# Background transfers kept back around a block exchange, and a high/low split placed later, in a one-core convolution and mixer kernel

## Chip, core and metric

The kernel runs on one core of a Trainium2 chip. The core has five engines with a queue each: TensorE (matmuls), VectorE, ScalarE, GpSimd and SyncE. SyncE only issues DMAs; GpSimd here mostly does so too. An engine takes its instructions in order and waits at the head of its queue. The metric is the device time of one execution, in microseconds (us); lower is better.

## The reference

Input `x` has 8 batches of 4096 tokens with 192 channels. A causal convolution with 7 softmax-normalised taps per head (8 heads of 24 channels) is followed by a token mixer and a channel mixer:

```python
w = softmax(weight)                        # 8 heads x 7 taps
xc = sum_k w[h, k] * x_pad[:, s + k, h, :]   # 6 zero rows ahead of each batch
xt = xc.transpose(0, 2, 1)
h = maximum(xt @ w_tok1, 0) @ w_tok2       # 4096 -> 256 -> 4096 tokens
u = xc + h.transpose(0, 2, 1)
out = u + maximum(u @ w_ch1, 0) @ w_ch2    # 192 -> 1536 -> 192 channels
```

## The kernel before

**Groups and tiles.** The batches form five groups, `[0], [1], [2, 3], [4, 5], [6, 7]`. A group's convolution and first token product ("stage 1", `stage1`) run as background while earlier groups go through the rest. The rest is done in tiles of 512 tokens (four blocks of 128), eight tiles a group. Products are made from high and low parts (a rounded copy and the remainder), so most operands exist as a `hi`/`lo` pair.

**A tile of a group of two batches.** For each of its batches (`i` = 0, 1), `channel1` makes 1536 hidden rows for the 512 tokens: six pairs of PSUM banks, 18 matmuls a pair (L971), each bank turned by ScalarE into a high part (L1010) and by VectorE into a low part (L1011). Then channel2 (`channel2_halves` for batch 0, `channel2` for batch 1) makes four output blocks; VectorE adds them to `u` (L1034/L1036, L1049/L1050), and `store_out` sends the tile (L1057, GpSimd's queue). All of these take PSUM banks from one pool of six, `ps_x`, so a bank that VectorE frees late stops the matmul that needs it next.

**The turn.** Within the second batch of a tile the next tile is prepared. After `channel1`, `mix2` makes the second token product of the next tile; VectorE adds it to `u` (L886) and transposes 32x32 blocks (L887). `blocks_sent` then moves these blocks between partitions with 16 DMAs of 48 KB (L920), eight from SyncE's queue and eight from GpSimd's. `parted` waits for them: ScalarE casts the high part (L933, three instructions), VectorE makes the low part (L935, three), ScalarE copies both to the upper half of `other` (L938, two), and GpSimd's queue copies the lower halves (L940, two DMAs). The first channel1 of the next tile reads the first four results at once; the DMA'd halves are read by the second batch's channel1. Before the change, `parted` stands between the second and the third of channel2's four blocks. There are 24 such turns: the last tile of group 1 and all tiles of groups 2 to 4 but the very last.

**The background.** A planner (`Background`) weaves stage 1 into this program at the time it is written. It keeps two estimated clocks, `pe` and `dve`, in nanoseconds. Each foreground step calls `bg.fg(pe, dve, after)`: it advances `pe`, pops background items in `fill` until the estimated VectorE clock is more than `after` ahead of TensorE's, then charges the step's own VectorE time. An item has a cost, a lag behind the item before it, and a gate that can hold it back. Its place in the program is thus decided by estimates, and the engines keep that order whatever the real times are.

**Stage 1 of a pair of batches.** It goes in four sections of 1024 tokens (`q2` = 0 to 3). Each section's rows are loaded in two halves of the channels (`begin`, `load`: two DMAs of 672 KB on SyncE's queue at L622; for section 0 also a memset by GpSimd behind each load, L624). The taps are VectorE instructions over 24 channels (L634, in twos), with the first tap a scale on ScalarE (L632). `store` sends the result with two DMAs on GpSimd's queue (L658). Mixing splits the result (L706 ScalarE, L710 VectorE) and multiplies it on TensorE into `ps_a` (L726 to L728). A section's first tap has a gate: its rows must be marked as loaded, some microseconds must have gone by on the estimated clock (10,000 ns for section 0, else 6,000 for two batches), and the split of the section two before must have been popped. The first half of the next section is loaded while the second half of this one is convolved, and the second half after that.

```python
def begin(q2, part):
    states[q2]["raw", part] = load(q2, part)
    mark("load", q2, part)

def loaded(q2, part):
    at = done.get(("load", q2, part))
    return None if at is None or pools(q2 % 2) is None else at + (2e3 + 2e3 * nb if q2 else 10e3)
```

Of the kernel before, what the change touches and what calls it, by code (L numbers as in the profile page):

```python
# [15 lines left out]
GROUPS = [[0], [1], [2, 3], [4, 5], [6, 7]]  # L16
# [18 lines left out]
class Background:  # L35
# [6 lines left out]
    def __init__(self):  # L42
        self.streams = []
        self.tiled = False
        self.pe = 0.0
        self.dve = 0.0

    def add(self, items, lead=0.0, group=None):
        total = sum(it.cost for it in items) or 1.0
# [53 lines left out]
        self.pe = max(self.pe, self.dve)  # L103

    def finish(self, group=None):
        mine = [s for s in self.streams if s["group"] == group]
        while any(s["items"] for s in mine):
            for s in mine:
                while self.may(s):
                    self.pop(s)  # L110
        self.streams = [s for s in self.streams if s["items"]]
# [3 lines left out]
def conv_mixer_kernel(ctx: ExitStack, tc: tile.TileContext, x, weight, w_tok1, w_tok2, w_ch1, w_ch2, out):  # L115
    nc = tc.nc
# [17 lines left out]
    RB = 8  # L134
# [7 lines left out]
    def f32(ap):  # L142
# [8 lines left out]
    bg = Background()  # L151
# [10 lines left out]
    xcd = [  # L162
        dram.tile([P, len(g), NJ, D], F32, name=f"xcd{i}") for i, g in enumerate(GROUPS)
    ]
# [434 lines left out]
    def stage1(gi, pools):  # L599
        bs = GROUPS[gi]  # L600
        nb = len(bs)
# [36 lines left out]
        states = [{} for _ in range(NS)]  # L638
        done = {}

        def mark(*key):
            done[key] = max(bg.pe, bg.dve)

        def begin(q2, part):
            states[q2]["raw", part] = load(q2, part)
            mark("load", q2, part)

        def taps(q2, h, k):
            st = states[q2]
            if k == 0 and h == 0:  # L650
                st["xc"] = pools(q2 % 2).tile([P, RB * nb, D], F32, name=f"xc{q2 % 2}")
            for i in range(2):
                conv(st["raw", h // HH], st["xc"], h + i, k)

        def store(q2):
            xc = states[q2]["xc"].rearrange("p (j b) d -> p j b d", b=nb)
            for i in range(nb):
                nc.gpsimd.dma_start(out=xcd[gi][:, i, q2 * RB:(q2 + 1) * RB], in_=xc[:, :, i])  # L658
            mark("conv", q2)

        def t1_load(n):
# [176 lines left out]
    def tokens(u, i):  # L838
        return u[:, :, :, i]

    def rows(v):
        return v.rearrange("p (c d) -> p c d", d=D2)
# [193 lines left out]
                nc.vector.tensor_tensor(out=osb[:, j], in0=v, in1=osb[:, j], op=ALU.add)  # L1036
        bg.tiled = False

    def channel2(i, h, u, osb, js):
        for j in js:  # L1040
            ts = slice(j * P, (j + 1) * P)
            ps = ps_x.tile([P, TT], F32, name="ps_x")
            for n, f in enumerate(order):
                z = n == NF - 1
                nc.tensor.matmul(out=ps[:, :2 * D], lhsT=h["hh", f][:, ts], rhs=w2[:, f, :], start=n == 0, stop=False)  # L1045
                nc.tensor.matmul(out=ps[:, :D], lhsT=h["hl", f][:, ts], rhs=w2[:, f, :D], start=False, stop=z)  # L1046
                if n % 4 == 3:
                    bg.fg(1140, 660 if z else 0, 200)
            nc.vector.tensor_tensor(out=rows(osb[:, j]), in0=rows(ps[:, :D]), in1=tokens(u, i)[:, j], op=ALU.add)  # L1049
            nc.vector.tensor_tensor(out=osb[:, j], in0=ps[:, D:2 * D], in1=osb[:, j], op=ALU.add)  # L1050

# [110 lines left out]
    for gi, bs in enumerate(GROUPS):  # L1162
        nb = len(bs)
        last = gi + 1 == len(GROUPS)
        if gi == 0:
            starts[1] = stage1(1, lambda k: sp0)
            starts[1][0](sp0)
            first_items()
        elif not last:
            if gi + 1 not in starts:  # L1170
                starts[gi + 1] = stage1(gi + 1, lambda k: cps[k])
            starts[gi + 1][0](sp)
        if gi == 0:
            u, abc = first["u"][1], first["abc"]
            loaded = first["next"]
        for q in range(NT):
            nxt = (gi, q + 1) if q + 1 < NT else (gi + 1, 0)
            for i, b in enumerate(bs):
                turn = i == nb - 1 and nxt[0] < len(GROUPS)
                run_ahead(gi)  # L1180
                if turn and nxt[0] != gi:
                    starts[nxt[0]][1]()
                    if gi == 0:
                        stage_ctx.close()
                        t2s_ctx.close()
                        conv_pool(1)
                        sp = ctx.enter_context(tc.tile_pool(name="sp1", bufs=1, reuse_waits="tile"))
                    loaded = load_tile(*nxt, sp)
                half = range(0, TJ // 2), range(TJ // 2, TJ)
                ahead = gi or q  # L1190
                if ahead:
                    h = channel1(abc[i])
                    run_ahead(gi)
                    osb = hp.tile([P, TJ, D], F32, name="osb")
                else:
                    osb = first["osb"]
                    first_channel2(u, osb, half[0])
                pairs = len(GROUPS[min(nxt[0], len(GROUPS) - 1)]) > 1
                if turn and pairs:
                    z = up.tile([P, ND * NQ, P], F32, name="own_hi")  # L1200
                    mix2(*nxt, *loaded, turned=z)
                    other = blocks_sent(z)
                elif turn:
                    if gi == 0 and nxt[0] == 0:
                        bg.require(("t2", nxt[1] // 2, nxt[1] % 2))
                    mix2(*nxt, *loaded)
                    mixed[0] = nxt[1]
                product2 = channel2 if turn or last and q + 1 == NT and i + 1 == nb else channel2_halves
                if ahead:
                    product2(i, h, u, osb, half[0])  # L1210
                if turn:
                    abc = parted(other) if pairs else transposed(loaded[1])
                run_ahead(gi)
                if not ahead:
                    w2_split()
                if last and q + 1 == NT and i + 1 == nb:
                    for j in range(TJ):
                        if j in half[1]:
                            channel2(i, h, u, osb, [j])
                        store_out(gi, b, q, osb, range(j, j + 1), nc.sync)  # L1220
                else:
                    if ahead:
                        product2(i, h, u, osb, half[1])
                    else:
                        first_channel2(u, osb, half[1])
                    store_out(gi, b, q, osb, range(TJ), nc.gpsimd)
                if not ahead:
                    ht_ctx.close()
                    hp = ctx.enter_context(tc.tile_pool(name="hp", bufs=1, reuse_waits="tile"))
                if turn:  # L1230
                    u = loaded[1]
                    if nxt[1] + 1 < NT:
                        loaded = load_tile(nxt[0], nxt[1] + 1, sp)
# [31 lines left out]
```

## Time and profile before

| | |
|---|---|
| runs shown (us) | 2060.33, 2061.2, 4994.83 |
| median | 2061.2 |
| profiled execution, its own time | 2060.38 |
| its span in the profile | 2058.6 |
| DMA moved | 258.39 MB, mean 126 GB/s |
| raw-row loads (L622) | 56, median 7.0 us from issue to landing |
| convolution stores (L658) | 28, median 8.1 us |
| block DMAs (L920) | 384, median 2.2 us on SyncE's queue, 2.0 on GpSimd's |
| lower halves (L940) | 48, median 3.5 and 4.9 us |

The span is the time from the first instruction to the last, and 1.8 us of the execution's own time lie around it. Groups 0 and 1 take about the first 600 us. The tiles of groups 2 to 4 follow; stage 1 of groups 3 and 4 runs beside the first twelve or so of them, to about 1380 us, and the tiles after that have no background at all.

In the rows quoted below, `x` and a number give how many instructions a group holds. A time-order row reads: start and duration in us, engine (SPq is SyncE's queue), line, operation, `out<-in`, shapes, and in brackets how long the engine stood idle before it and what ended that. A row of waits reads: who waited for whom, us in total, times, longest. A row of stretches reads: from and to, length, then for TensorE's matmuls, its weight loads, VectorE, ScalarE and GpSimd the busy time and the number of instructions, then TensorE's granted clock (1.00 is full), the DMA engines' busy share and GB/s.

### The profile page before, as it was taken

The page shows a single profiled execution, that of the slowest core. Times are in us where ns is not written, and L with a number is a line of the kernel's source. Part 1 is how long each engine was busy: PE and PEld are TensorE (multiplying, and loading weights), DVE is VectorE, ACT ScalarE, POOL GpSimd, SP SyncE. Part 2 cuts the span into 40 slices and gives each one's busy share as a digit, 9 for nine tenths or more (in the row PEclk, how much of TensorE's full clock was granted, in tenths as well). Part 3 has the DMA queues.
Part 4 walks back from the last instruction along what each step waited for, and adds up shares of the span by engine and source line. Part 5 has one row for each costly group of instructions (what it writes and reads, how often), then busy time and mean ns, then how long its engine had stood idle before and what let it go on. Part 6 is the DMA issues. An engine that isn't in the chain of part 4 may idle for free.

```text
span 2058.6 us, 41998 instructions
## 1 busy us (share of the span) xinstructions
PE 2030.5 (99%) x17435; PEld 1885.0 (92%) x17435; DVE 1450.9 (70%) x2877; ACT 761.2 (37%) x1305; POOL 218.7 (11%) x383
## 2 busy tenths in 40 slices
PE   9999999999999999999999998999999999999999
PEld 9789999998989888999999997999999999999998
DVE  7899989999558987756985688645555455555554
ACT  4575534434333333333333323332233322333222
POOL 0100000000011011101111110111010111111110
PEclk9999999999999999999999999999999999999999
DMA  9845446554364466324553343532222332333310
GB/s 310 291 157 168 131 146 192 181 166 135 132 172 121 134 187 173 91 84 135 159 167 113 111 127 102 146 93 61 64 60 74 83 83 77 81 83 83 83 47 17
DMA packets 289230, 258.39 MB, mean 126 GB/s; under 512 B 209360, under 2 KB 238544, under 8 KB 289040
## 3 DMA queue, kind: packets, MB, share of 16 engines
q1 hardware_dynamic: 265120, 168.00, 28.4%
q0 software_dynamic: 23920, 87.71, 14.0%
q8 instruction: 138, 2.26, 0.4%
q14 instruction: 52, 0.43, 0.1%
HBM read 146.60 MB, written 71.30 MB: 106 GB/s over the span
## 4 chain that ended last, share of the span: by engine, by line
PE 84%; DVE 8%; ACT 3%; DMA 2%; SPq 2%; issue 1%; POOL 0%; ACTq 0%; DVEq 0%
PE ps_x L971 34%; PE ps_x L1045 15%; PE ps_x L1028 15%; PE ps_x L1046 7%; DVE xc L634 4%; PE ps_x L871 2%; PE ps_x L873 1%; PE ps_x L872 1%; DVE hl L1011 1%; PE ps_a L726 1%; PE ps_a L727 1%; PE ps_a L728 1%; SPq L920 1%; DMA dec_raw<-in_moe_w_tok_dram 1%; PE ps_a L427 1%; PE ps_x L868 1%
## 5 line engine op out<-in xcount | busy, mean ns | idle before, releaser
L1010 ACT ACTIVATE hh<-ps_x 128x512 fp32r<-128x512 f32 x756 | 410.6, 596 | 758.7 <-PE ps_x L971 758.6
L1011 DVE SCALAR_TENSOR_TENSOR hl<-ps_x,hh 128x512 fp32r<-128x512 f32 x756 | 483.2, 683 | 192.6 <-ACT hh L1010 191.6
L1045 PE MATMUL ps_x<-w,hh 128*128 128x384 f32 x1872 | 539.2, 360 | 0.1
L1046 PE MATMUL ps_x<-w,hl 128*128 128x192 f32 x1872 | 469.2, 251 | 0.0
L971 PE MATMUL ps_x<-other,w_hi 64*128 64x512 f32 x1728 | 454.6, 390 | 6.6 <-DVE osb L1050 6.0
L634 DVE SCALAR_TENSOR_TENSOR xc<-raw,cw,xc 128x384 f32<-128x384 f32 (+1 forms) x768 | 388.0, 559 | 14.2 <-ACT xc L632 14.2
L1046 PEld LDWEIGHTS ps_x<-w,hl 128*128 128x128 f32 x1872 | 358.7, 192 | 0.0
L1045 PEld LDWEIGHTS ps_x<-w,hh 128*128 128x128 f32 x1872 | 352.1, 188 | 0.7 <-DVE hl L1011 0.7
L971 PEld LDWEIGHTS ps_x<-other,w_hi 64*128 64x128 f32 x1728 | 313.0, 184 | 34.5 <-issue 5.9
L971 PE MATMUL ps_x<-own_hi,w_hi 64*128 64x512 f32 x1440 | 337.4, 395 | 2.8 <-DVE hl L1011 1.6
L1028 PE MATMUL ps_x<-w,hh 64*128 64x384 f32 x2304 | 331.4, 356 | 0.0
L971 PE MATMUL ps_x<-own_hi,w_lo 64*128 64x512 f32 x1440 | 325.7, 387 | 0.0
L971 PE MATMUL ps_x<-own_lo,w_hi 64*128 64x512 f32 x1440 | 325.3, 387 | 0.0
L1028 PE MATMUL ps_x<-w,hl 64*128 64x192 f32 x2304 | 307.2, 247 | 0.1
L1028 PEld LDWEIGHTS ps_x<-w,hl 64*128 64x128 f32 x2304 | 248.5, 188 | 1.1 <-DVE hl L1011 0.6
L1028 PEld LDWEIGHTS ps_x<-w,hh 64*128 64x128 f32 x2304 | 245.6, 184 | 0.7
L971 PEld LDWEIGHTS ps_x<-own_hi,w_hi 64*128 64x128 f32 x1440 | 208.4, 184 | 37.8 <-DVE hl L1011 7.0
L971 PE MATMUL ps_x<-other,w_lo 64*128 64x512 f32 x864 | 242.4, 387 | 0.0
L971 PEld LDWEIGHTS ps_x<-own_hi,w_lo 64*128 64x128 f32 x1440 | 215.3, 184 | 25.7 <-DVE w_lo L187 0.5
L971 PEld LDWEIGHTS ps_x<-own_lo,w_hi 64*128 64x128 f32 x1440 | 215.4, 184 | 24.8
L971 PEld LDWEIGHTS ps_x<-other,w_lo 64*128 64x128 f32 x864 | 159.3, 184 | 11.9
L1049 DVE TENSOR_TENSOR osb<-ps_x,u 128x192 f32<-128x192 f32 x156 | 55.1, 353 | 144.8 <-PE ps_x L1046 144.4
(143 smaller groups left out, 2157.3 us busy)
## 6 DMA issues: line engine op xcount, KB each, us to landing
raw<-in_x_dram SPq DMA_DIRECT2D x56, 672.0 KB, 7.0
t<-t2d SPq DMA_DIRECT2D x64, 512.0 KB, 5.1
out_dram<-osb POOLq DMA_DIRECT2D x63, 384.0 KB, 4.6
u<-xcd SPq DMA_DIRECT2D x62, 384.0 KB, 6.0
xcd<-xc POOLq DMA_DIRECT2D x28, 768.0 KB, 8.1
t<-t1p SPq DMA_DIRECT2D x32, 512.0 KB, 5.0
other<-own_hi SPq DMA_DIRECT2D x192, 48.0 KB, 2.2
other<-own_hi POOLq DMA_DIRECT2D x192, 48.0 KB, 2.0
```

The lines of the kernel that those rows point to most:

```text
L427: nc.tensor.matmul(out=accs[kc][:, :D], lhsT=tops[i][:, c0:c0 + P], rhs=xcs[j // NC][:, j % NC], start=j == 0, stop=j == NJ - 1,)
L634: nc.vector.scalar_tensor_tensor(out=dst, in0=src, scalar=cw[:, h, k:k + 1], in1=dst, op0=ALU.mult, op1=ALU.add)
L726: nc.tensor.matmul(out=ps, lhsT=wh, rhs=xh, start=a, stop=False)
L727: nc.tensor.matmul(out=ps, lhsT=wh, rhs=xl, start=False, stop=False)
L871: nc.tensor.matmul(out=ps[:, :n], lhsT=wh, rhs=hh, start=a, stop=False)
L971: nc.tensor.matmul(out=ps, lhsT=w1[w][rows, c, p * P:(p + 1) * P], rhs=t[h][v][rows, c], start=n == 0, stop=n == len(prods) - 1,)
L1010: nc.scalar.activation(out=h["hh", f], in_=ps, func=AF.Relu)
L1011: nc.vector.scalar_tensor_tensor(out=h["hl", f], in0=ps, scalar=0.0, in1=f32(h["hh", f]), op0=ALU.max, op1=ALU.subtract)
L1028: nc.tensor.matmul(out=ps[:, :m], lhsT=h[part, f][ks, ts], rhs=w2[ks, f, :m], start=n == 0 and part == "hh", stop=z and part == "hl",)
L1045: nc.tensor.matmul(out=ps[:, :2 * D], lhsT=h["hh", f][:, ts], rhs=w2[:, f, :], start=n == 0, stop=False)
L1046: nc.tensor.matmul(out=ps[:, :D], lhsT=h["hl", f][:, ts], rhs=w2[:, f, :D], start=False, stop=z)
L1049: nc.vector.tensor_tensor(out=rows(osb[:, j]), in0=rows(ps[:, :D]), in1=tokens(u, i)[:, j], op=ALU.add)
```

## The change

Two things are altered. First, `Background` gets a list of held transfers. `begin` and `store` hand their DMAs to `transfer`, which issues them at once, or puts them on the list while a hold is on. In each of the 24 turns a hold begins ahead of the second batch's `channel1` and ends behind `blocks_sent`, where the list is issued in its order. A load counts as marked only when it is issued. If a section's first tap is about to reuse a result buffer whose store is still held, the list is issued there; `finish` issues it too. Second, in those turns `parted` is called from within `channel2`, after eight of the twelve steps of the third token block (`n` = 7 of `j` = 2), and no longer ahead of that block. Turns that prepare a group of one batch are as before.

```diff
+    def transfer(self, fn):
+        if self.held is None:
+            fn()
+        else:
+            self.held.append(fn)
+
+    def hold(self):
+        if self.held is None:
+            self.held = []
+
+    def release(self):
+        fns, self.held = self.held or [], None
+        for fn in fns:
+            fn()
...
     def finish(self, group=None):
+        self.release()
...
         def begin(q2, part):
-            states[q2]["raw", part] = load(q2, part)
-            mark("load", q2, part)
+            def fn():
+                states[q2]["raw", part] = load(q2, part)
+                mark("load", q2, part)
+
+            bg.transfer(fn)
...
             if k == 0 and h == 0:
+                if done.get(("storing", q2 - 2)):
+                    bg.release()
                 st["xc"] = pools(q2 % 2).tile([P, RB * nb, D], F32, name=f"xc{q2 % 2}")
...
         def store(q2):
             xc = states[q2]["xc"].rearrange("p (j b) d -> p j b d", b=nb)
-            for i in range(nb):
-                nc.gpsimd.dma_start(out=xcd[gi][:, i, q2 * RB:(q2 + 1) * RB], in_=xc[:, :, i])
+
+            def fn():
+                for i in range(nb):
+                    nc.gpsimd.dma_start(out=xcd[gi][:, i, q2 * RB:(q2 + 1) * RB], in_=xc[:, :, i])
+                done["storing", q2] = False
+
+            done["storing", q2] = True
+            bg.transfer(fn)
             mark("conv", q2)
...
-    def channel2(i, h, u, osb, js):
+    def channel2(i, h, u, osb, js, at=None):
...
                 if n % 4 == 3:
                     bg.fg(1140, 660 if z else 0, 200)
+                if at and at[0] == (j, n):
+                    at[1]()
...
+                pairs = len(GROUPS[min(nxt[0], len(GROUPS) - 1)]) > 1
+                if turn and pairs:
+                    bg.hold()
                 if ahead:
                     h = channel1(abc[i])
...
                     mix2(*nxt, *loaded, turned=z)
                     other = blocks_sent(z)
+                    bg.release()
...
-                if turn:
-                    abc = parted(other) if pairs else transposed(loaded[1])
+                if turn and not pairs:
+                    abc = transposed(loaded[1])
...
                     if ahead:
-                        product2(i, h, u, osb, half[1])
+                        if turn and pairs:
+                            made = []
+                            channel2(i, h, u, osb, half[1], ((half[1][0], 7), lambda: made.extend(parted(other))))
+                            abc = made
+                        else:
+                            product2(i, h, u, osb, half[1])
```

More of the change, by code (lines that the diff above doesn't have):

```diff
@@ L46, in __init__ @@
         self.dve = 0.0
+        self.held = None
+    def transfer(self, fn):
[10 more added lines that the diff above has]
+            fn()
     def add(self, items, lead=0.0, group=None):
@@ L1197, in conv_mixer_kernel @@
                     first_channel2(u, osb, half[0])
-                pairs = len(GROUPS[min(nxt[0], len(GROUPS) - 1)]) > 1
                 if turn and pairs:
```

## The prediction

> **What bounds the kernel now.** I read the page first (busy shares and the 40 slices), then the table of stretches with one row for each tile of the groups of two batches, then TensorE's waits, then the time order of each engine around single turns.
>
> ```profile
> PE 2030.5 (99%) x17435; PEld 1885.0 (92%) x17435; DVE 1450.9 (70%) x2877; ACT 761.2 (37%) x1305; POOL 218.7 (11%) x383
> ```
>
> TensorE is the bound: busy 99% of the span. No edit here takes a matmul away, so only TensorE's waits can go. The rows below show how large they are; each stretch runs from one tile's first channel1 matmul to the next tile's.
>
> ```profile
> core 0 of [0], span 2058.6 us
> core 0: us, PE busy (x) PEld busy (x) DVE busy (x) ACT busy (x) POOL busy (x), PEclk, DMA share, GB/s
> 606.82:666.55 59.73, 57.70 (x529) 52.76 (x528) 54.15 (x109) 19.98 (x36) 6.18 (x12) 1.00 0.40 115
> 666.55:735.75 69.20, 66.50 (x577) 61.19 (x576) 60.23 (x118) 29.00 (x48) 10.55 (x17) 1.00 0.57 165
> 735.75:809.02 73.27, 68.09 (x578) 62.34 (x578) 57.69 (x112) 24.81 (x41) 8.33 (x14) 0.98 0.61 167
> 809.02:876.16 67.14, 66.26 (x578) 60.39 (x577) 54.41 (x106) 22.81 (x37) 8.34 (x14) 1.00 0.39 114
> 876.16:940.89 64.73, 64.73 (x577) 63.37 (x576) 33.55 (x63) 19.97 (x32) 6.55 (x12) 1.00 0.36 101
> ...
> 1176.48:1250.26 73.78, 67.73 (x577) 62.36 (x576) 56.47 (x110) 24.81 (x41) 8.33 (x14) 0.95 0.53 145
> 1250.26:1317.35 67.09, 66.24 (x577) 60.70 (x577) 54.39 (x106) 22.80 (x37) 8.34 (x14) 1.00 0.39 112
> ...
> 1382.08:1438.49 56.41, 56.41 (x529) 55.05 (x529) 29.94 (x59) 17.53 (x29) 6.54 (x12) 1.00 0.25 68
> ```
>
> A tile of 529 matmuls takes 56.41 us with no convolution beside it; one of 577, with the next group's mixing in it, takes 64.73 us. What a row has above that is waiting: 3.3, 4.5, 8.5, 2.4, 9.1 and 2.4 us in the six rows that exceed it, 30.2 us together. That is the most the change can win in these rows, 1.5% of the time. The waits name VectorE:
>
> ```profile
> PE ps_a L727 <- DVE xhl L710: 9.9, 2, 5.8
> PE ps_x L971 <- DVE osb L1050: 6.0, 5, 2.2
> ```
>
> I number turns from 0 (blocks of the first tile of group 2, sent at 595 us); turn 3 ends in the row at 735.75, turn 10 in the one at 1176.48. Turn 10 shows both waits. The rows are SyncE, GpSimd, ScalarE, VectorE, TensorE, and the granted clock after the wait.
>
> ```profile
> 1223.27 6.40 SPq L622 DMA_DIRECT2D raw<-in_x_dram  x2
> 1230.02 10.12 SPq L920 DMA_DIRECT2D other<-own_hi  x8
> ```
> ```profile
> 1221.00 1.79 POOL L658 DMA_DIRECT2D xcd<-xc  x2 [12.96 <-DVE xc L634]
> 1226.80 3.81 POOL L920 DMA_DIRECT2D other<-own_hi  x7 [4.01 <-issue]
> ```
> ```profile
> 1241.99 1.66 ACT L933 CAST own_hi<-other 128x512 fp32r<-128x512 f32 x3 [18.33 <-DMA other<-own_hi]
> ```
> ```profile
> 1242.64 1.89 DVE L935 TENSOR_TENSOR own_lo<-other,own_hi 128x512 fp32r<-128x512 f32 x3 [10.18 <-ACT own_hi L933]
> 1244.46 0.95 DVE L710 TENSOR_TENSOR xhl<-xc,xhl 128x768 fp32r<-128x768 f32 x1
> ...
> 1247.20 7.50 DVE L634 SCALAR_TENSOR_TENSOR xc<-raw,cw,xc 128x384 f32<-128x384 f32 x14 [1.14 <-ACT xc L632]
> ```
> ```profile
> 1245.46 0.69 PE L727 MATMUL ps_a<-xhl,t 128*128 128x384 f32 x1 [5.81 <-DVE xhl L710]
> ```
> ```profile
> 1247.00:1249.00 2.00, 2.00 (x8) 2.00 (x7) 1.80 (x4) 2.00 (x5) 0.00 (x0) 0.52 0.82 184
> ```
>
> The chain: two raw-row loads hold SyncE for 6.40 us and two stores precede GpSimd's block DMAs; the blocks are issued slowly (10.12 us for eight) and land at about 1241.9. ScalarE then casts the high part, VectorE, idle 10.18 us at the head of its queue, makes the low part, and only behind it stand L710, for which TensorE waits 5.81 us, and 14 convolution taps (0.54 us each), behind which the last L1049/L1050 frees a PSUM bank late. After the wait TensorE restarts at a granted clock of 0.52, so the wait costs more than its idle time.
>
> **The change part by part.** (1) *The hold.* Raw loads and stores that the planner would issue from the turn's channel1 to `blocks_sent` go to a list and out behind the blocks, on the same queues. No DMA is added or removed. In turns 3 and 10 the blocks then stand first. Turn 11 is the nearest row: two xcd stores, but no raw load, stood before the blocks there.
>
> ```profile
> 1300.92 5.93 SPq L920 DMA_DIRECT2D other<-own_hi  x8
> ```
> ```profile
> 1310.31 1.66 ACT L933 CAST own_hi<-other 128x512 fp32r<-128x512 f32 x3 [11.89 <-DMA other<-own_hi]
> ```
>
> Its cast starts 9.4 us after SyncE's first block. In turn 10 SyncE's first block could go at about 1226.2 (GpSimd, free of its queue, has its first at 1226.80), so the cast would start at 1235.6, 6.4 us earlier, and own_lo would end near 1238.2, before the second mixing product needs its operand at 1239.6 (1245.46 less 5.81). The wait and its slow restart go. What is moved: the raw loads are the second half of the next section, first read after 24 pairs of taps (48 x 0.54 = 26 us of VectorE), so their lateness of some 9 us is covered; the stores are read one group later. GpSimd's two low-half copies (L940) now have the stores (1.79 us) ahead, but they wait for ScalarE's cast anyway, and their reader is channel1 of the tile's second batch, some 26 us after the first's (12.2 of channel1, 13.7 of channel2 by the planner's numbers). If that cover were gone, 1.8 us a turn in four turns. In turns 6 and 7 a first-half load moves too; its taps stand behind half a section of others, so I cost it at nothing.
>
> (2) *The parting stands later.* `parted` moves from the middle of channel2 to eight of twelve steps into its third token block, 2.28 us by the planner's 1,140 ns per four steps. Nothing of channel2 lies between on ScalarE or VectorE, so in a turn without background work the order on both stays the same and the cost is nothing. I check the cover there:
>
> ```profile
> 1490.62 1.67 ACT L933 CAST own_hi<-other 128x512 fp32r<-128x512 f32 x3 [12.56 <-DMA other<-own_hi]
> 1492.32 1.48 ACT L938 CAST other<-own_hi 64x1536 fp32r<-64x1536 f32 x1
> 1493.71 1.46 ACT L938 CAST other<-own_lo 64x1536 fp32r<-64x1536 f32 x1
> ```
> ```profile
> 1494.88 0.49 PE L971 MATMUL ps_x<-own_hi,w_hi 64*128 64x512 f32 x1
> ```
>
> The cast waits for the landing, not for its place; the high copy is ready 1.08 us before channel1, and the low one (1495.17) 1.07 us before its first use, six of nine products (1.36 us) into it. With background work, the planner's fills at steps 4 and 8 of the third block now come first. Before, three `bg.fg(0, 700, 0)` put the planner's VectorE clock 2.1 us ahead at the end of the second block, so those fills gave nothing. Now step 4 pops the second L710 and step 8 the first scale (L632) and a pair of taps: they run in the time in which VectorE stood idle for own_hi. The run of 14 taps becomes about 12 and starts 2 to 3 us earlier. Turn 10: own_lo to 1238.2, evacuation 0.7, 12 taps 6.4, evacuation 0.7: 1246.0, against a channel1 that would start at 1250.26 - 7.7 = 1242.6 and needs the bank two pairs (2 x 2.04 us by the planner) later, at 1246.7. That wait goes; the low parts behind it leave about 0.5.
>
> (3) *Turn 0.* Here the hold catches the first loads of group 3's convolution, which were sent before the blocks.
>
> ```profile
> 569.93 11.14 SPq L622 DMA_DIRECT2D raw<-in_x_dram  x4
> ...
> 595.22 5.22 SPq L920 DMA_DIRECT2D other<-own_hi  x8
> ```
> ```profile
> 581.61 0.57 POOL L624 MEMSET raw<- 1x576 f32 x1 [0.92 <-DMA raw<-in_x_dram]
> ...
> 585.75 0.57 POOL L624 MEMSET raw<- 1x576 f32 x1 [1.31 <-DMA raw<-in_x_dram]
> ```
> ```profile
> 604.02 0.54 POOL L940 DMA_DIRECT2D other<-own_hi  x1 [3.91 <-ACT own_hi L933]
> ```
>
> The first half landed 11.7 us after its first issue. Now SyncE is free at 600.4 and it lands at about 612.1 (611 if less contended). The planner lets the first tap go 10 us after the marked load, in the last quarter of channel2, so ScalarE's scale stands before channel1's relus and blocks ScalarE until 612.7; four taps (2.2) and the evacuation (0.7) end near 616, and channel1 from 606.82 needs that bank at 610.9. That is a wait of about 5 us in place of the 3.3 that this row loses now: I take +1.4. Bounds: -3.3 (it lands in time) and +5.7 (as late as the fourth load, 15.8 us after issue). GpSimd's memsets, now ahead of L940, hold that queue until about 616 instead of 604; the copies are read some 26 us after 606.82, so nothing, and one for one beyond that.
>
> Sum, by rows: 666.55 loses 4.0 of its 4.5, 735.75 all 8.5, 809.02 all 2.4, 1176.48 all 9.1, 1250.26 1.9 of 2.4; less 1.4 for turn 0: 25.8 - 1.4 = 24.4 us. The profiled execution took 2060.38 us (span 2058.6); the median of the runs shown is 2061.2, 0.8 above. 2060.4 - 24.4 = **2036.0**.
>
> **The rivals.** *Only the late blocks are cured.* The taps keep their run of 14 and the PSUM waits stay, because the fills give VectorE the same work just ahead of channel1. Then the two L710 waits go, 9.9 us, with the slow restarts (about 3): 2060.4 - 12.9 = 2047.5. For it: the number of taps is the same; against it: VectorE's idle time ahead of own_lo, which the new place fills.
>
> *The transfers still collide.* The released loads and stores start while the blocks are in flight, and the landings stay where they are; then rows 735.75 and 1176.48 keep the 12.9 and the gain is 24.4 - 12.9 = 11.5: 2048.9. Against it: in turn 11, with the stores ahead of the blocks, they were cast 9.4 us after issue, against 12.0 in turn 10. The Trainium skill (DMA: Bandwidth & Descriptors, "Issuing engines are not separate DMA queues" and "Queues, rings and completion order") says that all queues run on the same 16 engines, which take turns between queue rows packet by packet, so what is released on one queue shares with blocks still moving on the other. By it this rival is possible; no run here yet shows released transfers behind blocks.
>
> *The delay moves on.* If several loads land late as in turn 0, half of the gain is given back: about 2056.
>
> *Slower: the split is late at every turn.* If its new place (2.28 us later), not the landing, set its end, channel1 would wait 2.28 - 1.07 = 1.2 us in each of 24 turns: 2060.4 + 29 = 2089. It decides once the parting ends 1.07 us later than now; slower by 2% needs 2.8 us in every turn. Against it: nothing on ScalarE waits for channel2 there.
>
> **How the numbers follow.** Forecast 0.60; only the late blocks 0.13; collision 0.09; delay moved on 0.12; slower 0.06. The low end is 2060.4 - 30.2 = 2030; the high end, 2053, takes in the first two rivals and turn 0's bound on one of them. That leaves out the last two, 0.18. About 2% (41 us) can be told from no change: more than the 30.2 of all six rows, so faster 0.02; slower 0.03, half of the last rival; same 0.95.
>
> **What would show it.** Right: L622 and L658 behind L920 in turns 3 and 10, own_hi 6 us sooner after the transposes, no L710 wait of TensorE, a second L710 before own_lo on VectorE, the rows at 64.7. Turn 0's scale should wait for its load. Wrong: L920 still issued over 10 us, runs of 14 taps, or channel1 starting over 1 us late in the turns after 1382 us.

## The result, and the profile after

The changed kernel takes 2047.59 us (median; 2046.94 to 2049.57), the kernel before 2061.32 us on the same chip: a ratio of 0.9937, 95% interval 0.9917 to 0.9956, so 13.7 us saved. One of the four executions of the kernel before took 4994.83 us, and the ratio leaves it out. The forecast was 2036.0 us within 2030 to 2053, and "same" by the 2% bound. The time lies in that range and the change counts as "same", but only about half of the 24.4 us that it summed arrived. The profiled execution took 2047.31 us (span 2045.5); the rows below are from it.

The page of the changed kernel, first part: the busy times of the engines. Below it, from the same kernel, the answer on TensorE's waits (engine, line waited for, total us, times, longest).

```profile
PE 2023.1 (99%) x17435; PEld 1858.9 (91%) x17435; DVE 1453.1 (71%) x2877; ACT 761.7 (37%) x1305; POOL 219.6 (11%) x383
```
```profile
PE ps_x L999 <- DVE osb L1080: 10.5, 4, 4.4
PE ps_x L999 <- DVE hl L1039: 1.4, 2, 1.1
```

The instructions are the same in number. The wait of the second mixing product (9.9 us of L727 for L710 before, now L755 for L738) is gone from the list. But the wait of channel1 for a PSUM bank (L971 for L1050 before, now L999 for L1080) has grown from 6.0 us in five to 10.5 us in four. The table of stretches says where; again one row for each tile, from one tile's first channel1 to the next.

```profile
core 0 of [0], span 2045.5 us
607.00:667.50 60.50, 58.60 (x529) 52.19 (x528) 53.56 (x107) 19.98 (x37) 8.87 (x17) 1.00 0.57 156
667.50:735.80 68.30, 66.70 (x579) 60.32 (x578) 57.06 (x110) 26.20 (x43) 10.68 (x17) 1.00 0.52 154
735.80:810.84 75.04, 67.26 (x577) 62.24 (x576) 64.22 (x125) 28.33 (x47) 8.39 (x14) 0.95 0.57 162
810.84:875.58 64.74, 64.74 (x578) 60.01 (x578) 52.48 (x101) 22.94 (x37) 8.40 (x14) 1.00 0.49 138
...
1175.05:1239.78 64.73, 64.73 (x577) 60.00 (x576) 57.47 (x112) 24.97 (x41) 8.39 (x14) 1.00 0.54 151
1239.78:1304.52 64.74, 64.74 (x578) 60.01 (x578) 52.48 (x101) 22.95 (x37) 8.39 (x14) 1.00 0.49 137
...
1369.25:1425.64 56.39, 56.39 (x530) 51.66 (x530) 29.97 (x59) 17.45 (x29) 6.57 (x12) 1.00 0.24 67
```

Against 56.41 and 64.73 us without a wait, the six rows now exceed by 4.1, 3.6, 10.3, 0, 0 and 0 us: 18.0 where it was 30.2. That is 12.2 of the 13.1 us by which the span shrank; the other 0.9 lies in small differences elsewhere. Rows four to six, the turns 3 and 10 with their late blocks, are clean. The third row, which was to lose 8.5 us, became 1.8 us longer. It begins with the channel1 behind turn 2 and ends with turn 3, so the gain at its end (turn 3's 4.1 us wait for L710 is gone) is paid back, and more, at its start.

**Where it worked.** Turn 10 of the changed kernel in order of time, all engines but TensorE (start, duration, engine and line, count, idle time before and its releaser):

```profile
1223.33 5.11 SPq L948 DMA_DIRECT2D other<-own_hi  x8
1223.98 4.36 POOL L948 DMA_DIRECT2D other<-own_hi  x8 [19.05 <-DMA t<-t1p]
...
1228.34 1.83 POOL L682 DMA_DIRECT2D xcd<-xc  x2
1228.55 3.58 SPq L639 DMA_DIRECT2D raw<-in_x_dram  x2
...
1229.55 0.95 DVE L738 TENSOR_TENSOR xhl<-xc,xhl 128x768 fp32r<-128x768 f32 x1
...
1231.18 3.27 DVE L651 SCALAR_TENSOR_TENSOR xc<-raw,cw,xc 128x384 f32<-128x384 f32 x6 [0.68 <-ACT xc L649]
1232.58 1.65 ACT L961 CAST own_hi<-other 128x512 fp32r<-128x512 f32 x3
```

Loads and stores (L639, L682) stand behind the blocks (L948), which SyncE now issues in 5.11 us and not in 10.12. The high cast starts 8.60 us after GpSimd's first block; before it was 15.19 (1241.99 less 1226.80). VectorE makes the second low part L738 and six taps ahead of `own_lo`, in time in which it stood idle before.

**Where it failed.** Turn 2, in the same view, with SyncE, GpSimd, ScalarE and VectorE, then TensorE's two long waits:

```profile
724.94 14.45 SPq L639 DMA_DIRECT2D raw<-in_x_dram  x4
...
725.51 0.93 POOL L682 DMA_DIRECT2D xcd<-xc  x1 [1.14 <-DVE osb L1079]
...
727.55 0.89 POOL L682 DMA_DIRECT2D xcd<-xc  x1 [1.11 <-issue]
```
```profile
729.62 1.47 ACT L966 CAST other<-own_lo 64x1536 fp32r<-64x1536 f32 x1
739.88 2.13 ACT L649 ACTIVATE xc<-raw,cw 128x384 f32<-128x384 f32 x4 [8.79 <-DMA raw<-in_x_dram]
```
```profile
740.52 2.21 DVE L651 SCALAR_TENSOR_TENSOR xc<-raw,cw,xc 128x384 f32<-128x384 f32 x4 [11.44 <-ACT xc L649]
```
```profile
743.54 0.47 PE L999 MATMUL ps_x<-own_hi,w_hi 64*128 64x512 f32 x1 [3.36 <-DVE osb L1080]
...
748.43 0.76 PE L999 MATMUL ps_x<-other,w_hi 64*128 64x512 f32 x1 [4.42 <-DVE osb L1080]
```

The first two of the four DMAs at 724.94 are a first-half load. In the kernel before, it went out at 694.93, 2.1 us ahead of the channel1 with which the hold now begins:

```profile
694.93 1.24 SPq L622 DMA_DIRECT2D raw<-in_x_dram  x2
```

In the changed program it falls into the hold and goes out 30 us later. The planner has by then put the scale (L649) that reads it ahead of channel1's relus, and ScalarE executes in order: it stands idle for 8.79 us, VectorE behind it for 11.44, the evacuations (L1079, L1080) behind VectorE's taps come late, and TensorE waits 3.36 and 4.42 us for their banks and then runs slowly for some microseconds. The channel1 behind turn 2 lasts 22.5 us, not about 12.4.

### The profile page after: what moved, and what is told of

It is laid out like the page before. It is cut to its first block, busy times and chain, and to the rows that moved or that the text cites. A ratio compares the mean times of both kernels' runs of the same rounds, so it can differ in the third digit from the quotient of the medians.

```text
span 2045.5 us, 42015 instructions
## 1 busy us (share of the span) xinstructions
PE 2023.1 (99%) x17435; PEld 1858.9 (91%) x17435; DVE 1453.1 (71%) x2877; ACT 761.7 (37%) x1305; POOL 219.6 (11%) x383
## 4 chain that ended last, share of the span: by engine, by line
PE 89%; DVE 5%; DMA 3%; ACT 1%; SPq 1%; issue 0%; POOL 0%; ACTq 0%; POOLq 0%; DVEq 0%
PE ps_x L999 36%; PE ps_x L1073 16%; PE ps_x L1056 16%; PE ps_x L1074 7%; DVE xc L651 2%; PE ps_x L899 2%; PE ps_a L754 2%; PE ps_a L755 2%; PE ps_a L756 2%; PE ps_x L901 1%; PE ps_x L900 1%; DVE hl L1039 1%; DMA raw<-in_x_dram 1%; PE ps_a L444 1%; DMA dec_raw<-in_moe_w_tok_dram 1%; PE ps_x L896 1%
## 5 line engine op out<-in xcount | busy, mean ns | idle before, releaser
L999 PE MATMUL ps_x<-other,w_hi 64*128 64x512 f32 x1728 | 452.7, 390 | 7.4 <-DVE osb L1080 7.2
L999 PEld LDWEIGHTS ps_x<-other,w_hi 64*128 64x128 f32 x1728 | 314.7, 185 | 43.7 <-issue 8.3
L999 PE MATMUL ps_x<-own_hi,w_hi 64*128 64x512 f32 x1440 | 335.4, 394 | 5.7 <-DVE osb L1080 3.4
L999 PE MATMUL ps_x<-own_hi,w_lo 64*128 64x512 f32 x1440 | 326.2, 387 | 0.0
L999 PE MATMUL ps_x<-own_lo,w_hi 64*128 64x512 f32 x1440 | 326.1, 387 | 0.0
L1056 PE MATMUL ps_x<-w,hl 64*128 64x192 f32 x2304 | 291.7, 247 | 0.1
L999 PEld LDWEIGHTS ps_x<-own_hi,w_hi 64*128 64x128 f32 x1440 | 209.8, 184 | 40.5 <-issue 9.9
L999 PE MATMUL ps_x<-other,w_lo 64*128 64x512 f32 x864 | 242.8, 387 | 0.0
L999 PEld LDWEIGHTS ps_x<-own_hi,w_lo 64*128 64x128 f32 x1440 | 215.7, 184 | 27.5 <-DVE w_lo L204 0.5
L999 PEld LDWEIGHTS ps_x<-own_lo,w_hi 64*128 64x128 f32 x1440 | 215.8, 184 | 26.6
L1056 PEld LDWEIGHTS ps_x<-w,hl 64*128 64x128 f32 x2304 | 225.0, 188 | 1.8 <-DVE hl L1039 0.9
L1056 PEld LDWEIGHTS ps_x<-w,hh 64*128 64x128 f32 x2304 | 221.4, 184 | 0.9
L999 PEld LDWEIGHTS ps_x<-other,w_lo 64*128 64x128 f32 x864 | 159.4, 184 | 18.0
L1079 DVE TENSOR_TENSOR osb<-ps_x,u 128x192 f32<-128x192 f32 x156 | 55.4, 355 | 144.8 <-PE ps_x L1074 144.3
```

The costliest lines, as they stand in the source:

```text
L999: nc.tensor.matmul(out=ps, lhsT=w1[w][rows, c, p * P:(p + 1) * P], rhs=t[h][v][rows, c], start=n == 0, stop=n == len(prods) - 1,)
L1056: nc.tensor.matmul(out=ps[:, :m], lhsT=h[part, f][ks, ts], rhs=w2[ks, f, :m], start=n == 0 and part == "hh", stop=z and part == "hl",)
```

## The experiments

Three theories stood at the start. A: the hold cures the late blocks of turns 3 and 10, the later parting cures the waits of turns 0 to 2, and the two together lose where a first-half load is held. B: the loss in turn 2 comes from the later place of the parting. C: the hold gives nothing.

### Each part alone

The changed kernel with the parting at its old place, so that only the hold is left:

```diff
-                if turn and not pairs:
-                    abc = transposed(loaded[1])
+                if turn:
+                    abc = parted(other) if pairs else transposed(loaded[1])
```

> The hold alone; the parting stands where it stood before. Theory A (the hold cures the late blocks, the later place cures the rest, and the 10 us that turn 2 now loses come from a first-half raw load that was held there): the blocks of turns 3 and 10 land 12 us after the first transpose, the two waits of TensorE for the split convolution result (9.9 us and their slow restarts, 12.9 together) go, the runs of 14 taps and the waits for a PSUM bank behind them stay; in this program no raw load falls into turn 2's hold, so that turn waits about 2.4 us as before. Time 2047 to 2050. Theory B (the turn-2 loss is made by the later place of the parting, and the hold is harmless): the same here. Theory C (the hold gives nothing by itself because the released transfers collide with the blocks): 2058 to 2062.

Measured: 2049.62 us, ratio 0.9946 (0.9931 to 0.9961). Three rows of its table of stretches (they begin with the channel1 behind turns 1, 2 and 9, and end with turns 2, 3 and 10):

```profile
668.10:737.38 69.28, 66.75 (x578) 61.41 (x577) 60.37 (x118) 28.88 (x48) 10.42 (x17) 1.00 0.59 166
737.38:804.86 67.48, 66.62 (x578) 60.62 (x578) 58.27 (x114) 24.83 (x41) 8.37 (x14) 1.00 0.57 160
...
1172.59:1239.18 66.59, 66.24 (x577) 60.69 (x576) 57.49 (x112) 24.84 (x41) 8.36 (x14) 1.00 0.50 143
```

No L738 wait is left, so the late blocks are cured. Turns 0 and 1 keep excesses as before (3.8 and 4.6 us), and the rows behind turns 2, 3, 9 and 10 keep 1.9 to 2.8 us each. Behind turns 0 and 1 the waits name the bank that VectorE frees late (1.1 and 2.1 us); behind turn 2 they do so for 0.6 us, and in the other three rows for none, so that the taps make what stays there is argued and not shown. In this kernel turn 2's first-half load still goes out ahead of the hold, at 696.37: it takes both edits to bring it into the hold. This is the program of the first rival, in which only the late blocks are cured, and it comes within 2.1 us of that rival's 2047.5.

The changed kernel without the hold, so that only the later parting is left:

```diff
-                if turn and pairs:
-                    bg.hold()
```

> The later parting alone; nothing is held. Theory A: the second low part of the split stands ahead of the parting on VectorE, so TensorE's wait for it goes even with blocks that land late; in turns 3 and 10 the late blocks then cost 1 to 4 us at channel1, and no scale waits for a held load, so turn 2 has no stall. Time 2038 to 2046, that is not slower than with both parts. Theory B: the stall of 10 us in turn 2 is there as well, and the time is 2050 or more. Theory C: all of the gain stands here, 2045 to 2048.

Measured: 2038.68 us, ratio 0.9896 (0.988 to 0.9913). In this kernel every first-half load goes out as before, and the rows that begin behind turns 0 to 2 are clean (56.39, 64.74, 64.71 us). Turns 3 and 10 keep a wait; SyncE, ScalarE and TensorE in turn 10:

```profile
1206.59 6.38 SPq L639 DMA_DIRECT2D raw<-in_x_dram  x2
1213.33 10.09 SPq L948 DMA_DIRECT2D other<-own_hi  x8
```
```profile
1225.28 1.66 ACT L961 CAST own_hi<-other 128x512 fp32r<-128x512 f32 x3 [6.45 <-DMA other<-own_hi]
```
```profile
1228.49 0.79 PE L999 MATMUL ps_x<-other,w_hi 64*128 64x512 f32 x1 [2.05 <-ACT other L966]
```

The blocks are as late as in the kernel before, but `own_lo` no longer stands ahead of L738 on VectorE, so the second mixing product isn't held up. The lateness now reaches TensorE through the upper-half copies (L966), with 2.05 us here. So the later parting alone removes the 9.9 us wait, and so does the hold alone. Put on top of the later parting, the hold makes the kernel 8.9 us slower (2047.59 less 2038.68). B and C fall: turn 2 is clean with the later parting alone, and the hold alone gains 11 us.

### First-half loads, free or gated later

The changed kernel, with first-half loads never held:

```diff
-            bg.transfer(fn)
+            if part:
+                bg.transfer(fn)
+            else:
+                fn()
```

> Both parts, but the load of a section's first half is never held (second halves and stores are). Theory A: turn 2 loses its 10 us and turn 0 its wait, ScalarE's scale finds its rows landed; turns 3 and 10 stay cured: 2033 to 2037. Theory B: turn 2 stays as it is with both parts, 2045 to 2049.

Measured: 2030.07 us (2029.88 to 2030.96), ratio 0.9852 (0.9838 to 0.9867), some 3 us below the range that was expected. From its table of stretches, the first three rows and the one that ends with turn 10:

```profile
607.49:663.87 56.38, 56.38 (x529) 51.68 (x529) 52.85 (x106) 21.30 (x38) 9.89 (x17) 1.00 0.55 147
663.87:728.59 64.72, 64.72 (x578) 60.05 (x577) 61.00 (x119) 27.09 (x44) 8.44 (x15) 1.00 0.64 178
728.59:793.30 64.71, 64.71 (x577) 60.04 (x576) 57.70 (x113) 25.67 (x42) 8.37 (x14) 1.00 0.60 169
...
1157.69:1222.42 64.73, 64.73 (x577) 60.04 (x576) 57.47 (x112) 24.94 (x41) 8.36 (x14) 1.00 0.55 151
```

PE busy equals the length of every row: all 30.2 us of the six rows are gone. The 17.5 us between this kernel and the changed one are, within half a microsecond, the 18.0 us of excess in the first three rows of the changed one. Turns 0, 1 and 2 are all lost to held first-half loads, turn 1 by way of turn 0: the convolution starts later, and its first scale, ahead of the parting here, stands behind it on ScalarE there.

The other way round, with all loads held, but a held load marked 18 us later, so that the planner lets its taps go later:

```diff
+            kept = bg.held is not None
...
                 mark("load", q2, part)
+                if kept:
+                    done["load", q2, part] += 18e3
```

> Both parts, all held as in the change, but a load that was held counts as marked 18,000 ns later on the planner's clock, so that its taps are not placed before it has landed. Theory A: ScalarE no longer waits for the load in turn 2 and turn 0; the taps come later as background: 2034 to 2041. Theory B: 2045 to 2049. If the loss were the sharing of the DMA engines itself, whatever the place of the scale, it stays near 2047 too.

Measured: 2031.67 us, ratio 0.986 (0.9845 to 0.9874), better than expected. The row behind turn 2 is clean (64.72 us; the rows ahead of it 57.03 and 65.44). The load still goes out behind the blocks, and the scale now stands in the middle of channel1, behind relus that it would have blocked. But its company is gone too, since the whole convolution comes later. SyncE and GpSimd in turn 2 of this kernel:

```profile
719.07 1.28 SPq L639 DMA_DIRECT2D raw<-in_x_dram  x2
```
```profile
733.31 0.91 POOL L686 DMA_DIRECT2D xcd<-xc  x1 [1.53 <-DVE xc L651]
```

The first store starts 14 us behind the load, and the second-half load at 734.11. The load's two DMAs land 5.0 and 7.2 us after their issue, where the second one of the changed kernel takes 14.5. So this run shows that a late issue need not cost anything; whether the scale's place or the missing company cures turn 2, it can't say.

### Why the held load lands so late

In turn 2 the scale starts 14.9 us after the first issue of its load (739.88 less 724.94), where the page of the profile gives a raw load a median of 7.2 us from issue to landing. Beside it move the second-half load and two stores. Three kernels change that company. In the first, held second-half loads go to a second list (`late`), which is issued behind the parting:

```diff
-            bg.transfer(fn)
+            bg.transfer(fn, part == 1)
...
-                            channel2(i, h, u, osb, half[1], ((half[1][0], 7), lambda: made.extend(parted(other))))
+                            channel2(i, h, u, osb, half[1], ((half[1][0], 7), lambda: (made.extend(parted(other)), bg.release_late())))
```

> The changed kernel, but of what is held only the first-half loads and the stores go out behind the blocks; the second-half loads wait on until the parting. In turn 2 the held first-half load then goes out without the second-half load beside it. If the company of the transfers is what makes turn 2 late (14.5 us from issue to landing), it lands some 7 to 9 us after its issue, ScalarE's scale starts 5 to 7 us sooner, the row that takes 75.04 us in the changed kernel comes to 65 to 69, and the time to 2038 to 2042. If the late issue alone is the cause, the row stays over 73 us and the time is 2045 to 2048.

Measured: 2047.82 us, ratio 0.9932 (0.9915 to 0.9948). In the second, stores are never held:

```diff
             done["storing", q2] = True
-            bg.transfer(fn)
+            fn()
```

> The changed kernel, but the stores are never held: all raw loads go out behind the blocks, the stores ahead of them as the planner would have them. If the two stores beside the four loads of turn 2 are what slows these, the first-half load lands some 10 us after its issue instead of 14.5 and the row of 75.04 us loses 4 us or more: 2041 to 2044. If it is the loads among themselves, or the late issue, the row stays over 73 us: 2046 to 2048. The blocks of turns 3 and 10 should come in time in both cases.

Measured: 2047.51 us, ratio 0.9934 (0.9919 to 0.9949). Both look like a verdict against the company, but their traces show that neither changed it. SyncE in turn 2, in the first and in the second of these kernels:

```profile
724.06 15.54 SPq L646 DMA_DIRECT2D raw<-in_x_dram  x4
```
```profile
722.16 15.18 SPq L639 DMA_DIRECT2D raw<-in_x_dram  x4
```

The four DMAs still go out together: the planner asks for the second-half load only behind the release, and as nothing that waits stands between the two on SyncE's queue, it is issued at once. The two stores also come from the planner behind the blocks, held or not. These two runs say nothing on the cause in turn 2. The third kernel is made so that the stores must move: from `bg.hold()` until the parting all stores go to the second list, and so out behind the parting's low-half copies, which wait for ScalarE.

```diff
-            bg.transfer(fn)
+            bg.transfer(fn, True)
...
-                            channel2(i, h, u, osb, half[1], ((half[1][0], 7), lambda: made.extend(parted(other))))
+                            channel2(i, h, u, osb, half[1], ((half[1][0], 7), lambda: (made.extend(parted(other)), bg.release_late())))
```

> The changed kernel, but from the hold of a turn on stores go out only behind the two low-half copies of the parting, which wait for ScalarE; in turn 2 GpSimd then issues them some 4 us later than the first-half load, not 0.1 to 2 us. All loads go as in the changed kernel. If the stores' bytes are what holds the first-half load up (14.5 us to the landing of its second DMA), it lands 8 to 10 us after its issue, the row of 75.04 us comes to 67 to 71, and the time to 2040 to 2044. If the second-half load behind it on the same queue, or the time of issue alone, does it, the landing stays over 13 us, the row over 73, and the time at 2046 to 2048.

Measured: 2039.53 us (2038.04 to 2041.18), ratio 0.9897 (0.988 to 0.9913). SyncE, GpSimd and ScalarE in turn 2 of this kernel, and the row that took 75.04 us:

```profile
724.93 7.13 SPq L649 DMA_DIRECT2D raw<-in_x_dram  x4
```
```profile
731.14 0.94 POOL L693 DMA_DIRECT2D xcd<-xc  x1
```
```profile
732.09 2.14 ACT L659 ACTIVATE xc<-raw,cw 128x384 f32<-128x384 f32 x4
```
```profile
735.86:802.89 67.03, 66.64 (x579) 60.34 (x578) 61.14 (x119) 25.68 (x42) 8.40 (x14) 1.00 0.63 176
```

The load is issued at the same time, but the stores come 5.6 us later (731.14, not 725.51). The scale starts 7.2 us after the issue, right behind ScalarE's copies, without a wait, and the row loses 8.0 us. The load's second DMA lands 6.6 us after its issue, not 14.5. So the stores' bytes beside the load made 8.0 of the 10.3 us lost there; at most the other 2.3 are left for the later issue by itself, and no run divides them. The Trainium skill ("DMA: Bandwidth & Descriptors", "Issuing engines are not separate DMA queues") states that DMAs run on the same 16 DMA engines whichever engine started them. The trace agrees: stores from GpSimd's queue set when a load from SyncE's queue lands.

### Which of the held transfers made the blocks late

With the later parting, two kernels hold one kind only. One theory: the raw load ahead of the blocks on SyncE's queue makes them late. The other: the stores do. First only the stores held (loads: `fn()` in place of `bg.transfer(fn)`), then only the second-half loads:

> The later parting, and of the transfers only the convolution stores are held; no raw load is. With nothing held the later parting left waits of 3.6 and some 4.7 us at channel1 behind turns 3 and 10, where two second-half raw loads and two stores go ahead of the blocks. Theory S (the raw loads on SyncE's own queue make the blocks late there, the stores do little): both waits stay in the main, 2036 to 2039. Theory T (the stores on the other queue make them late): both go, 2030 to 2032.

Measured: 2031.0 us, ratio 0.9861 (0.9846 to 0.9875); three executions took 2030.93 to 2031.02 us, and the profiled one 2036.50. In that one turn 10 still waits:

```profile
PE ps_x L999 <- ACT other L966: 2.0, 1, 2.0
```

> The later parting, and only the second-half raw loads are held; first halves and stores are not. Theory S: the blocks of turns 3 and 10 land about 14 us after the first transpose, as in turn 11 before the change, and TensorE does not wait: 2030 to 2033. Theory T: 2036 to 2039.

Measured: 2029.67 us, ratio 0.9855 (0.9838 to 0.9872), with all rows clean in the profiled execution, and one of four executions at 2036.59. Neither theory holds alone: it mostly takes both transfers to make the blocks late, and moving either one is mostly enough. In the profiled execution above, the raw load alone was enough. Each kernel had one execution of four that was 5 to 8 us longer; the kernel with both held and free first halves had none in four. That is too few to say that holding both is safer.

### How much room the parting has

With first-half loads free, the parting at the end of the third block (all twelve steps), and then after eight steps of the fourth block:

```diff
-                            channel2(i, h, u, osb, half[1], ((half[1][0], 7), lambda: made.extend(parted(other))))
+                            channel2(i, h, u, osb, half[1], ((half[1][0], 11), lambda: made.extend(parted(other))))
```

> As the kernel with first halves free, but the parting stands at the end of the third token block (step 12 and not 8). If the time is set by what stands ahead of the parting on VectorE and the place has slack: 2029 to 2032. If the place is at its edge, the copies end up to 1.1 us later in the turns with background and channel1 waits there: 2032 to 2042.

Measured: 2030.34 us, ratio 0.9851 (0.9837 to 0.9866): no difference to step eight.

```diff
-                            channel2(i, h, u, osb, half[1], ((half[1][0], 7), lambda: made.extend(parted(other))))
+                            channel2(i, h, u, osb, half[1], ((half[1][1], 7), lambda: made.extend(parted(other))))
```

> As the kernel with first halves free, but the parting stands after step 8 of the fourth and last token block. In a turn without background VectorE then frees the third block's bank ahead of the low part, which ends some 0.7 us later; 1.07 us of slack were read from the profile before the change, so those turns should stay at 56.4 us a tile and the loss, if any, lies in the turns with background, where taps stand ahead of the low part: 2030 to 2050. If the slack is less than read, all 24 turns lose: above 2040 with tiles over 56.6 us at the end.

Measured: 2052.91 us, ratio 0.996 (0.9946 to 0.9975). Its wait for the upper-half copies (L969 is L966 of the changed kernel):

```profile
PE ps_x L1002 <- ACT other L969: 13.3, 9, 2.1
```

Here the split is late in turns with background work beside it, by up to 2.1 us; turns without it stay at 56.4 us. This is the slower rival's mechanism, but one block later than the change puts it.

## Why the prediction was right and where it was wrong

- **The bound and its size.** Right. All the time to be won lay in six rows, 30.2 us; the kernel with free first halves wins it, and its 2030.07 us is the low end of the range.
- **The late blocks (part 1).** Right in turn 10: the cast was to come 6.4 us sooner and came 6.6 sooner against GpSimd's first block (8.60 and 15.19 us), and 9.25 us after SyncE's (9.4 forecast). The rows at 809.02, 1176.48 and 1250.26, with 13.4 of 13.9 us to go, lost all of it. In turn 3 the blocks also stood first, but not because anything was held there. The kernel whose stores are never held shows where the planner puts them (the second-half load is the item just ahead of them). GpSimd in its turn 3, then in its turn 10:

```profile
793.50 4.34 POOL L948 DMA_DIRECT2D other<-own_hi  x8 [19.91 <-DMA t<-t1p]
797.84 1.82 POOL L682 DMA_DIRECT2D xcd<-xc  x2
```
```profile
1216.54 1.78 POOL L682 DMA_DIRECT2D xcd<-xc  x2 [12.96 <-DVE xc L651]
1222.63 4.34 POOL L948 DMA_DIRECT2D other<-own_hi  x8 [4.31 <-issue]
```

In turn 3 they come behind the blocks without any hold, as in the changed kernel: the loads held in turns 0 and 2 had put the convolution later (its next first half goes out at 763.61, not at 755.36). With the first halves free, turn 3 is clean as well, and there the order does rest on its own hold: the stores go out at 781.85, behind the blocks that begin at 777.51, while with nothing held they go out ahead of them (771.29 and 777.36). One count in part 1 was off: a second half is first read after 12 pairs of taps, not 24, so 24 x 0.54 = 13 us of VectorE's work covers it, not 26. The cover held: in turn 10 of the changed kernel the load is issued at 1228.55 and first read at 1253.35 (L649).
- **The failed step: which transfers the hold would catch.** Part 1 said that the held raw loads are second halves, covered by 26 us of taps, and costed the first-half loads of turns 6 and 7 at nothing. It read the held set from the order of the program before. In turn 2 a first-half load was issued 2 us ahead of the later hold, and in the changed program the planner asks for it inside the hold. The row at 735.75, forecast to lose 8.5 us, gained 1.8. The 10.3 us of excess in that row are most of the 12.3 us by which the rows missed the forecast (18.0 us of excess where 5.7 was to stay). The mechanism was at hand: it is part 3's (ScalarE blocked by a scale ahead of its load), in another turn.
- **Turn 1.** Mis-sized: the row at 666.55 was to lose 4.0 us and lost 0.9. As turn 0's first load is held, the convolution starts later, and its scale and taps crowd just ahead of turn 1's channel1. With that load free the row is clean.
- **Turn 0 (part 3).** Right in kind: the scale waits for the held load. The price was +0.8 and not +1.4 us (a wait of 5 in place of 3.3, as the text has it, would have been +1.7), as the first half was in place sooner than the forecast 612.1. ScalarE in the changed kernel, in order of time:

```profile
609.40 2.14 ACT L649 ACTIVATE xc<-raw,cw 128x384 f32<-128x384 f32 x4 [2.29 <-POOL raw L641]
```

- **The later parting (part 2).** Right, and undervalued: it removes the second mixing product's wait without any hold, which the sum credited to the hold. Where the blocks are late, the lateness reappears as a wait of up to 2.05 us at channel1.
- **The rivals.** The time, 2047.59, equals the 2047.5 of "only the late blocks are cured", but not by that rival's way: the bank waits of turns 3 and 10 did go, and that rival's program is the hold alone, 2049.62. What happened is "the delay moves on": one more load, and not several, landed late as in turn 0, through transfers that collide, though not with the blocks. That rival's time was summed wrongly: half of 24.4 us given back is 2060.4 - 12.2 = 2048.2, not 2056. So the path that the kernel took stood among those that the range left out, and that the range holds the measured time all the same owes something to luck. "The split is late at every turn" did not occur.

## What to carry to other kernels

When transfers are held back, list what will be in the hold by the changed program's own order, and ask of each one which in-order engine executes its first reader and how soon; hold only what isn't read soon, or gate its reader later as well (2030.07 and 2031.67 us here). Look at what starts beside a released load: in turn 2 a second-half load and two stores, which the planner asked for later, started with it all the same, as nothing ahead of them on their queues waited, and the stores' bytes cost 8.0 us. Where two edits cure one wait, measure each alone: here either removes it, and the second one, put on top, cost 8.9 us until its held set was trimmed, after which both together gave 30.7 us (2060.76 to 2030.07).

## What the runs showed of the hardware

The DMA engines are full after the release in turn 2 of the changed kernel. The table of stretches shows it in its last two columns, the share of the 16 engines' time and GB/s; a share above 1 means that the packets' times, added up, exceed that time.

```profile
730.00:735.00 5.00, 5.00 (x34) 5.00 (x33) 0.00 (x0) 1.09 (x1) 0.00 (x0) 1.00 1.07 397
...
750.00:752.00 2.00, 2.00 (x13) 1.67 (x11) 2.00 (x5) 0.00 (x0) 0.00 (x0) 0.50 1.07 272
```

While the engines' time is all taken, SyncE itself is slow: the four loads keep it for 14.45 us, where it issues them in 7.13 us when the stores come later. The last row shows the granted clock at 0.50 behind the wait of 4.42 us. A shorter wait can be enough for that. In the kernel with the later parting alone, the wait of 2.05 us in turn 10 is followed by

```profile
1228.00:1230.00 2.00, 1.51 (x8) 1.23 (x10) 1.97 (x6) 1.98 (x3) 0.52 (x1) 0.58 0.99 351
1230.00:1232.00 2.00, 2.00 (x14) 1.58 (x12) 2.00 (x5) 1.41 (x2) 0.00 (x0) 0.56 1.13 348
1232.00:1234.00 2.00, 2.00 (x20) 1.66 (x18) 1.97 (x5) 1.09 (x2) 0.52 (x1) 1.00 1.02 200
```

so about 4 us at 0.57 of the clock, which by an estimate costs another 1.7 us (4 x 0.43), nearly as much as the wait itself. But not every such wait does it. In the kernel before, TensorE waits 2.21 us for a bank, until 673.37, and the clock stays whole:

```profile
673.00:675.00 2.00, 1.63 (x14) 1.62 (x16) 2.00 (x5) 0.65 (x2) 0.56 (x1) 1.00 1.00 259
```

The Trainium skill ("TensorE: Matmul & The Clock Gate", Part 1) names an idle window of about 3.4 us as what brings the half clock. Here the traces differ: 2.05 us of idle was followed by it and 2.21 us was not, so the length of the wait alone doesn't tell.
